# Two small VectorE jobs moved to GpSimd, and an earlier close for new VectorE cells, in a two-layer transformer kernel planned by a scheduler

**Chip, cores, metric.** One core of a Trainium2 chip. The metric is the device time of one execution in microseconds (us). "Ratio" below is the mean time of one kernel's fast runs over that of the other's of the same rounds, so it is not quite the ratio of the medians that are quoted.

## The reference

Two layers over x of 2048 rows by 512 columns; each is attention with 32 heads of 16, then an MLP of 1792 with a tanh GELU.

```python
x = x + _A_ref(_layernorm(x), A_wqkv, A_wo)              # attention
x = x + _B_ref(_layernorm(x), B_w1, B_b1, B_w2, B_b2)    # MLP
x = x + _A_ref(_layernorm(x), A_wqkv, A_wo)
x = x + _B_ref(_layernorm(x), B_w1, B_b1, B_w2, B_b2)

def _A_ref(x, wqkv, wo):                                 # cut
    scores = jnp.einsum("bhqd,bhkd->bhqk", q, k) * (Dh ** -0.5)
    p = _softmax(scores, axis=-1)
    o = jnp.einsum("bhqk,bhkd->bhqd", p, v)
    return o.transpose(...).reshape(B, S, D) @ wo
```

## The kernel before

A scheduler in the host program walks through generators ("threads") that yield operations with a modelled cost, keeps a modelled clock for each engine, and freezes one instruction order for each engine. Attention is cut into passes: eight heads' halves against a segment of 512 (at the end 256) queries. A pass has cells of 128 keys by 512 queries, in four columns (`a`). TensorE makes a cell's scores. Then either ScalarE takes the exponentials of two or three cells in one ACTIVATE, or VectorE makes one cell by an add-and-convert (`dfirst`) and two integer shifts (`dchain`): a "shift cell". Four PV matmuls use a shift cell, one uses a ScalarE cell. A pass accumulates in the one PV bank. The scheduler also books "fillers", matmuls whose result nobody uses, in gaps of TensorE.

The LN scale and shift, and the softmax normalisation at a pass's end:

```python
    def ln_tile(self, c, t, dst, dkeys, quick):
        ...
        yield _Op("dve", 0.4, lambda e: e.tensor_scalar(
            T["XLN"][:, x, :], T["X"][:, t, :], T["RSTD"][:, t:t + 1], T["NMR"][:, t:t + 1], op0=ALU.mult, op1=ALU.add),
            reads=["X.%d" % t, "RSTD.%d" % c, "NMR.%d" % c], writes=["XLN.%d" % x])
        if not quick:                       # a DMA transposes it; quick tiles go by TensorE
        ...
    def norm(self, l, seg, g, b, part, final):
        ...
        for i, t in enumerate(ts):
            o3 = T["OTT"][:, o, 0:w].rearrange("p (k c) -> p k c", c=32)[:, :, 16 * t:16 * t + 16]
            yield _Op("dve", 0.1 + 0.31 * w / 512, lambda e, i=i, o3=o3: e.tensor_tensor(
                out=o3, in0=x3[:, i * nb:i * nb + nb, 0:16],
                in1=T["RC"][:, i * nb:i * nb + nb, None].to_broadcast([128, nb, 16]), op=ALU.mult), ...)
```

Which cell VectorE gets next (`alist`, `dlist`: the pass's cells that ScalarE or VectorE may take; what is left of `dlist` when `alist` is empty goes to ScalarE too):

```python
    def next_d(self, used, start, pop=True):
        for pi in (self.pa, self.pa + 1):
            ...
            na = len(self.alist[pi])
            if pi == self.pa and na + len(self.dlist[pi]) < TAIL:      # TAIL = 10
                continue
            ...
```

An output tile of the MLP, named in the experiments:

```python
    def ytile(self, l, seg, t):
        tail = l == NL - 1 and seg[0] == self.NQ - 1
        ...
        b = None if tail else (yield ("need", ("w", l, seg, "2", (t, 0))))
        b = yield ("acq", "misc")
```

The softmax here doesn't subtract the row's maximum and nothing guards it: scores larger than these inputs give would overflow.

## Time and profile before

| before | |
|---|---|
| time | 1599.42 us (1598.87 to 1599.91, 3 runs); 1599.38 in the 6 runs beside the change |
| busy | ScalarE 1551.9 us (97%), TensorE 1431.5, VectorE 1360.6, GpSimd 115.7 |
| cells | 3221 in 1332 ACTIVATEs on ScalarE, 875 on VectorE |
| chain that ended last | ScalarE 72%, TensorE 25% |

ScalarE is the engine to watch. Its lines are in the prediction. I cut the span at its last exponential, a cut that the prediction did not make. Busy time by stretches (columns: stretch, length, then TensorE, its weight loads, VectorE, ScalarE and GpSimd busy with their instruction counts, granted clock, DMA), before:

```profile
80.00:1568.08 1488.08, 1332.56 (x17277) 410.33 (x17269) 1298.14 (x2489) 1468.96 (x1303) 89.71 (x106) 0.99 0.21 60
1568.08:1597.20 29.12, 23.33 (x530) 15.39 (x530) 8.94 (x22) 11.34 (x18) 1.07 (x2) 0.99 0.13 39
```

The span is 80 us of opening, the stretch to the last exponential (ScalarE busy 1469.0, idle 19.1 us), and a tail of 29.1 us in which TensorE has the most work. "Granted clock" is the share of its full clock that TensorE was given; what it looks like in the trace is told with the experiments.

### The profile page before, as it was taken

The page shows a single profiled execution, that of the slowest core. Times are in us where ns is not written, and L with a number is a line of the kernel's source. Part 1 is how long each engine was busy: PE and PEld are TensorE (multiplying, and loading weights), DVE is VectorE, ACT ScalarE, POOL GpSimd, SP SyncE. Part 2 cuts the span into 40 slices and gives each one's busy share as a digit, 9 for nine tenths or more (in the row PEclk, how much of TensorE's full clock was granted, in tenths as well). Part 3 has the DMA queues.
Part 4 walks back from the last instruction along what each step waited for, and adds up shares of the span by engine and source line. Part 5 has one row for each costly group of instructions (what it writes and reads, how often), then busy time and mean ns, then how long its engine had stood idle before and what let it go on. Part 6 is the DMA issues. An engine that isn't in the chain of part 4 may idle for free.

```text
span 1597.2 us, 42967 instructions
## 1 busy us (share of the span) xinstructions
PE 1431.5 (90%) x18762; PEld 449.4 (28%) x18762; DVE 1360.6 (85%) x2628; ACT 1551.9 (97%) x1391; POOL 115.7 (7%) x150
## 2 busy tenths in 40 slices
PE   8988889989899998999989988878998989888988
PEld 3222222222222222222222222222222222333344
DVE  6689998789998889978799788889878988997894
ACT  7999999999999999999999999989999999999995
POOL 4101010000000000000100010110000000000000
PEclk9999999999999999999999999999999999999999
DMA  5000001431115211142011510001251105313430
GB/s 146 15 2 1 2 14 48 133 81 41 25 50 147 60 35 28 48 146 67 28 34 41 172 41 28 1 1 34 70 170 30 33 14 156 97 35 101 140 81 29
DMA packets 141768, 96.90 MB, mean 61 GB/s; under 512 B 36877, under 2 KB 141582, under 8 KB 141582
## 3 DMA queue, kind: packets, MB, share of 16 engines
q1 hardware_dynamic: 141582, 94.14, 20.9%
q8 instruction: 150, 2.46, 0.6%
q14 instruction: 36, 0.29, 0.1%
HBM read 84.41 MB, written 2.10 MB: 54 GB/s over the span
## 4 chain that ended last, share of the span: by engine, by line
ACT 72%; PE 25%; DVE 2%; issue 0%; DMA 0%; POOL 0%; SPq 0%; ACTq 0%
ACT pt L1462 63%; PE ps L511 10%; PE ps L1134 8%; PE ps L1523 7%; ACT g L890 3%; ACT v L1462 2%; ACT kt L1462 1%; ACT q L1462 1%; ACT L890 1%; DVE du L1279 1%; ACT L1462 1%; DVE g L869 0%; PE ps L1122 0%; DVE kt L1279 0%; DMA x<-in_A_x_dram 0%
## 5 line engine op out<-in xcount | busy, mean ns | idle before, releaser
L1462 ACT ACTIVATE pt<-ps 128x1024 bf16<-128x1024 f32 (+1 forms) x1252 | 1377.9, 1260 | 16.0 <-PE ps L1134 7.3
L1134 PE MATMUL ps<-qp,kt 32*128 32x512 bf16 x4096 | 536.5, 385 | 146.9 <-ACT pt L1462 102.9
L1279 DVE TENSOR_SCALAR du<-ps 128x512 uint16<-128x512 f32 x705 | 477.5, 686 | 103.1 <-PE ps L1134 96.8
L1523 PE MATMUL ps<-pt,v 128*17 128x512 bf16 (+1 forms) x3340 | 457.0, 360 | 1.3 <-DVE du L1340 0.6
L1134 PEld LDWEIGHTS ps<-qp,kt 32*128 32x128 bf16 x4096 | 141.1, 91 | 693.2 <-ACT pt L1462 306.9
L1523 PE MATMUL ps<-du,vc 128*17 128x512 bf16 (+1 forms) x2370 | 327.9, 358 | 2.6 <-DVE du L1342 1.9
L1342 DVE TENSOR_SCALAR du<-du 128x2048 uint16<-128x2048 uint16 (+1 forms) x356 | 240.4, 680 | 1.9
L511 PE MATMUL ps<-xf,wr 128*32 128x512 bf16 (+1 forms) x2400 | 164.3, 368 | 1.1 <-DVE g L869 0.6
L1082 POOL TENSOR_SCALAR qp<-q,mask 128x512 bf16<-128x512 bf16 (+1 forms) x91 | 68.5, 753 | 1261.2 <-PE ps L1134 1252.4
L1523 PEld LDWEIGHTS ps<-pt,v 128*17 128x17 bf16 x3340 | 119.5, 89 | 118.5 <-issue 80.7
L1523 PE MATMUL ps<-du,v 128*17 128x512 bf16 (+1 forms) x790 | 149.4, 361 | 0.2 <-DVE xt L741 0.2
L1340 DVE TENSOR_SCALAR du<-du 128x1024 uint16<-128x1024 uint16 (+1 forms) x356 | 144.9, 419 | 1.8
L511 PE MATMUL ps<-wr,g 128*32 128x512 bf16 x1600 | 123.8, 382 | 4.4 <-ACT g L890 2.4
L1523 PEld LDWEIGHTS ps<-du,vc 128*17 128x17 bf16 x2370 | 91.2, 89 | 61.6 <-issue 25.8
L869 DVE TENSOR_SCALAR g<-ps,hb1t 128x512 bf16<-128x512 f32 (+1 forms) x112 | 79.9, 714 | 15.4 <-PE ps L511 13.9
L1523 PE MATMUL ps<-dh,vc 128*17 128x512 bf16 (+1 forms) x303 | 85.0, 359 | 0.0
L1279 DVE TENSOR_SCALAR dh<-ps 128x512 uint16<-128x512 f32 x90 | 61.7, 685 | 9.1 <-PE ps L1134 8.0
L511 PEld LDWEIGHTS ps<-xf,wr 128*32 128x32 bf16 x2400 | 51.1, 95 | 62.5 <-issue 34.2
L1279 DVE TENSOR_SCALAR kt<-ps 128x512 uint16<-128x512 f32 x80 | 54.9, 686 | 14.9 <-PE ps L1134 13.7
L1122 PE MATMUL ps<-vc 128*32 128x512 bf16 x564 | 60.0, 393 | 0.1
L1462 ACT ACTIVATE v<-ps 128x1536 bf16<-128x1536 f32 (+1 forms) x34 | 46.5, 1386 | 1.8 <-PE ps L1523 0.7
L1523 PEld LDWEIGHTS ps<-du,v 128*17 128x17 bf16 x790 | 37.5, 88 | 37.9 <-issue 21.1
(91 smaller groups left out, 1166.5 us busy)
## 6 DMA issues: line engine op xcount, KB each, us to landing
wr<-in_B_w_dram SPq DMA_DIRECT2D x256, 256.0 KB, 2.9
wr<-in_A_wqkv_dram SPq DMA_DIRECT2D x24, 256.0 KB, 2.9
wr<-in_A_wo_dram SPq DMA_DIRECT2D x18, 256.0 KB, 3.0
out_dram<-x SPq DMA_DIRECT2D x16, 128.0 KB, 2.7
g<-in_A_wqkv_dram SPq DMA_DIRECT2D x3, 512.0 KB, 6.0
x<-in_A_x_dram SPq DMA_DIRECT2D x3, 512.0 KB, 8.9
q<-in_B_w_dram SPq DMA_DIRECT2D x3, 512.0 KB, 5.5
kt<-in_B_w_dram SPq DMA_DIRECT2D x4, 256.0 KB, 3.5
```

The lines of the kernel that those rows point to most:

```text
L511: return [lambda e, a=a: e.matmul(out[32 * a:32 * a + 32, :], lhsT=lhsT[:, 32 * a:32 * a + 32], rhs=rhs, start=start, stop=stop, tile_posi ...
L869: yield _Op("dve", 0.21 + n / 966, lambda e, fc=fc, pb=pb: e.tensor_scalar(T["G"][:, fc, q], pb, T["HB1T"][:, fc:fc + 1], None, op0=ALU.ad ...
L890: lambda e, g=g: e.activation(out=g, in_=g, func=ACT.Gelu_apprx_tanh), reads=gk, writes=gk, prio=2)
L1082: yield _Op("pool", 0.1 + 0.6 * w / 512, lambda e, s=s, q=q, i=i, t=t, w=w: e.tensor_scalar(T["QP"][:, s, w * i:w * i + w], q, T["MASK"][: ...
L1122: fns.append(lambda e, o=o, w=w, a=a, m=m: e.matmul(o, lhsT=w, rhs=rhs, start=start, stop=start, tile_position=(0, m * a)))
L1134: return (lambda e: e.matmul(o, lhsT=lhsT, rhs=rhs, start=True, stop=True, tile_position=(32 * a, 0)), ["K%d.%d.%d" % (l, gb, kt // 4), "Q ...
L1279: yield _Op("dve", 0.68, lambda e: e.tensor_scalar(u, self.bank(b), E_SCALE, E_BIAS, op0=ALU.mult, op1=ALU.add), reads=["B.%d" % b], write ...
L1340: yield _Op("dve", 0.08 + 0.14 * n, lambda e: e.tensor_scalar(U[:, 1, 0:n, :], U[:, 0, 0:n, :], SHIFT, None, op0=ALU.add), reads=key[0], w ...
L1342: yield _Op("dve", 0.08 + 0.28 * n, lambda e: e.tensor_scalar(U[:, 2:4, 0:n, :], U[:, 0:2, 0:n, :], 2 * SHIFT, None, op0=ALU.add), reads=k ...
L1462: yield _Op("act", 0.065 + 0.4267 * n, lambda e, src=src, dst=dst: e.activation(out=dst, in_=src, func=ACT.Exp, scale=0.25), reads=["B.%d" ...
L1523: op.fns.append(lambda e, o=o, lhsT=q[0][0][m], rhs=q[0][1][:, n * m:n * m + n], a=a, st=st, sp=sp: e.matmul(o, lhsT=lhsT, rhs=rhs, start= ...
```

## The change

The intent: take two small jobs off VectorE so that it can take more cells from ScalarE, and stop shift cells from being opened late in a pass.

```diff
+OPENING = 18
-        yield _Op("dve", 0.4, lambda e: e.tensor_scalar(
+        eng, cost = ("dve", 0.4) if quick else ("pool", 0.72)
+        yield _Op(eng, cost, lambda e: e.tensor_scalar(            # LN scale and shift
...
+        pool = g < 6 and seg[2] == 512
-            yield _Op("dve", 0.1 + 0.31 * w / 512, lambda ...
+            yield _Op(*(("pool", 0.1 + 0.55 * w / 512) if pool else ("dve", 0.1 + 0.31 * w / 512)), lambda ...
...
-            if pi == self.pa and na + len(self.dlist[pi]) < TAIL:
+            left = [sum(x[2] == a for x in self.dlist[pi]) for a in range(4)]
+            if pi == self.pa and na + len(self.dlist[pi]) < (OPENING if min(left) == max(left) else TAIL):
                 continue
```

More of the change, by code (lines that the diff above doesn't have):

```diff
@@ L750, in norm @@
             o3 = T["OTT"][:, o, 0:w].rearrange("p (k c) -> p k c", c=32)[:, :, 16 * t:16 * t + 16]
-            yield _Op("dve", 0.1 + 0.31 * w / 512, lambda e, i=i, o3=o3: e.tensor_tensor(
+            yield _Op(*(("pool", 0.1 + 0.55 * w / 512) if pool else ("dve", 0.1 + 0.31 * w / 512)), lambda e, i=i, o3=o3: e.tensor_tensor(
                 out=o3, in0=x3[:, i * nb:i * nb + nb, 0:16],
```

## The prediction

> **What bounds the kernel now.** I read the page of the profile first: its busy shares, then the chain that ended last.
>
> ```profile
> PE 1431.5 (90%) x18762; PEld 449.4 (28%) x18762; DVE 1360.6 (85%) x2628; ACT 1551.9 (97%) x1391; POOL 115.7 (7%) x150
> ...
> ACT 72%; PE 25%; DVE 2%; issue 0%; DMA 0%; POOL 0%; SPq 0%; ACTq 0%
> ```
>
> ScalarE (ACT) works 97% of the span and carries 72% of the chain. GpSimd (POOL) is nearly empty. Next I cut the span into opening, middle and tail with the view of busy time by stretches (columns: PE, PEld, DVE, ACT, POOL).
>
> ```profile
> 0.00:80.00 80.00, 75.57 (x960) 23.64 (x963) 53.49 (x118) 71.57 (x72) 24.88 (x42) 1.00 0.31 80
> 80.00:1520.00 1440.00, 1290.23 (x16421) 388.67 (x16414) 1254.52 (x2398) 1420.95 (x1259) 89.71 (x106) 0.99 0.21 60
> 1520.00:1597.20 77.20, 65.67 (x1389) 37.06 (x1386) 52.56 (x114) 59.35 (x62) 1.07 (x2) 1.00 0.21 57
> ```
>
> ACT idles 8.4 us in the opening, 19.1 us in the 1440 us of the middle and 17.9 us in the tail: 45 us in all. The opening and the tail (a last MLP with no attention beside it) are not touched by the change. So the time is ACT's work plus about 45 us, and a change to another engine pays only if it takes work off ACT or shortens the 19 us. What ACT does in the middle, and what the other engines do for it, is in the groups by shape:
>
> ```profile
> L1462 ACT ACTIVATE pt<-ps 128x1024 bf16<-128x1024 f32 x763 | 802.7, 1093 | 7.2 <-PE ps L1134 4.0 <-PE ps L1523 2.0
> L1462 ACT ACTIVATE pt<-ps 128x1536 bf16<-128x1536 f32 x489 | 743.8, 1521 | 8.8 <-PE ps L1523 3.9 <-PE ps L1134 3.3
> L1279 DVE TENSOR_SCALAR du<-ps 128x512 uint16<-128x512 f32 x705 | 477.5, 686 | 103.1 <-PE ps L1134 96.8
> L1342 DVE TENSOR_SCALAR du<-du 128x2048 uint16<-128x2048 uint16 x349 | 237.4, 686 | 1.9
> L1340 DVE TENSOR_SCALAR du<-du 128x1024 uint16<-128x1024 uint16 x349 | 143.0, 422 | 1.8
> L1082 POOL TENSOR_SCALAR qp<-q,mask 128x512 bf16<-128x512 bf16 x75 | 59.5, 794 | 1074.8 <-PE ps L1134 1066.7 <-ACT q L667 7.9
> L600 DVE TENSOR_SCALAR xln<-x,rstd,nmr 128x512 bf16<-128x512 bf16 x64 | 25.7, 414 | 2.8 <-DMA kt<-xln 2.6
> L751 DVE TENSOR_TENSOR ott<-xt,rc 128x256 bf16<-128x256 f32 x56 | 23.2, 414 | 0.1
> ```
>
> There are 4096 cells of scores (128 keys by 512 queries). Each cell's exponential is made either by ACT (two or three cells per ACTIVATE) or by VectorE (DVE), with one add-and-convert from PSUM (L1279) and a share of two shift instructions (L1340, L1342) for the "shift cells". A scheduler in the host program decides cell by cell who takes it, from modelled costs and readiness. So freeing DVE pays by one road: the scheduler gives DVE more cells, and ACT has fewer. I counted the instructions of the two built programs, which is no timing. Before: 775 ACTIVATEs of two cells and 557 of three, so 3221 cells in 1332 instructions, and 875 on DVE. After: 793 of two, 540 of three and one of one, so 3207 cells in 1334 instructions, and 889 on DVE.
>
> [...] an undisturbed L1082 of 512 columns takes 0.69 us in the timeline. [...]
>
> [...] the same L1082 takes 0.69 us at 141 us and 2.07 us at 157 us, and its mean is 794 ns.
>
> ```profile
> 141.23 0.69 POOL L1082 TENSOR_SCALAR qp<-q,mask 128x512 bf16<-128x512 bf16 x1 [14.90 <-PE ps L1134]
> 157.10 2.07 POOL L1082 TENSOR_SCALAR qp<-q,mask 128x512 bf16<-128x512 bf16 x1 [15.18 <-PE ps L1134]
> ```
>
> [...]
>
> **The change, part by part.**
>
> (1) LN scale and shift to GpSimd. By the counts 58 of 64 L600 leave DVE: 58 x 0.414 = 24.0 us less on DVE, and 58 x 0.70 = 41 us more on GpSimd (estimate from L1082, same shape, one input). The six that stay are the quick ones at the start and the very end.
>
> (2) Softmax normalisation. 42 of the 56 L751 of 256 columns leave DVE: 42 x 0.414 = 17.4 us[...]. Passes 6 and 7 of a segment, behind which the output projection waits, and the half segments stay on DVE, so no longer latency stands where a segment ends. GpSimd goes from 116 to some 185 to 200 us, 12% of the span: it can't be a bound.
>
> (3) DVE takes 14 more cells: 14 x 0.686 = 9.6 us. By the counts the shift instructions become 3 more pairs (3 x 1.11 us) and 8 more singles (8 x 0.71 us): 9.0 us. DVE's sum: -41.4 + 18.6 = -23 us, so about 1338 us busy, with a lower share than now.
>
> (4) ACT, which decides. The slope from the two rows above: 1521 - 1093 = 428 ns per cell. All that ACT does besides exponentials (GELUs 53 us, 16 table loads of 1.283 us, some 8 us of copies) is about 82 us, so the exponentials take 1551.9 - 82 = 1470 us; less 3221 x 0.428 = 1379 us this leaves 91 us over 1332 instructions, 0.068 us each. The change is then -14 x 0.428 + 2 x 0.068 = **-5.9 us** on ACT. That lies on the path almost whole, since ACT is never out of work for long.
>
> (5) The opening rule. A DVE cell of the current pass may now be opened, when the four columns are level, only with 18 or more cells of the pass left, not 10. I built the two halves alone and counted. GpSimd's part alone puts 3205 cells in 1344 ACTIVATEs: -16 x 0.428 + 12 x 0.068 = -6.0 us. The opening rule alone gives ACT 9 cells more, in 3 instructions more: +4.1 us. Together they are worth the same as GpSimd's part alone, with 10 fewer ACTIVATEs and 2 cells more. So the rule buys nothing on ACT's work; if it buys anything, it is ACT's waits. A cell opened late holds the pass's single PV bank until its shift chain is done, so that PV matmuls and, behind them, the buffers that ACT writes into are late. Such waits are few: in ACT's waits between 30 and 1560 us, these two carry nearly all.
>
> ```profile
> ACT pt L1462 <- PE ps L1134: 7.3, 18, 0.8
> ACT pt L1462 <- PE ps L1523: 5.9, 3, 3.7
> ```
>
> The second is the kind the rule can help, 5.9 us in three waits. I take 1.5 us off, a choice, not a reckoning.
>
> (6) PE. Each cell on DVE needs four PV matmuls where one on ACT needs one: 42 more column matmuls, at 1431 / 18762 = 0.076 us about 3 us. Against it, 112 filler matmuls (L1122[...]) fall away, about 8.5 us. PE is 90% busy but loses work on balance, so it does not become the bound.
>
> Sum: 1599.4 - 5.9 - 1.5 = **1592 us**, 0.5% faster.
>
> **Rivals.**
>
> A. [...] For: shift instructions run 493 us (all shapes of L1340 and L1342), 31% of the span, 974 of them, so 0.61 start each us. [...] A delayed shift chain delays PV, and a delayed L1279 delays the score bank. Against: DVE loses 23 us of work[...]; it has 15% idle[...]. [...]
>
> B. *New waits of the frozen order.* Nearly every row of the order of instructions moves, so the 19 us of idle in the middle is drawn anew. GpSimd in its order serves the masked queries (L1082), which the next pass needs, behind an xln that itself may wait for statistics or its transpose's buffer. One such pile-up costs 1 to 3 us (the longest ACT wait now is 3.7 us). [...] Against: queries are made a pass or more ahead (three buffers). This makes 1592 plus or minus 5.
>
> C. *The rule works better than I grant*: it removes most of the 15 us that ACT waits in the middle, and frees PE. For: PE fillers fall from 1076 to 964 with both parts, while GpSimd's part alone keeps 1020, so the plan has fewer PE gaps. Against: fillers are not waits of ACT. It would give about 1584 us.
>
> **Range and chances.** The count of cells is sure, its price is measured, so -5.9 us is firm within 0.5 us; the rest is idle time on ACT, from -8 us (C) to +8 us (A with B). The eight-in-ten range is 1585 to 1599 us. Faster by over 2% would need 1567 us, more than all the idle time of the middle; slower by over 2% would need 38 us of new idle time on ACT. Both are very unlikely: 0.01 each, and 0.98 for within 2%.
>
> **What would show it.** Right: ACT busy near 1546 us, idle 42 to 45 us; DVE near 1338 us[...]; GpSimd 185 to 205 us; L600 on GpSimd at 0.70 to 0.95 us mean; ACT's wait for L1523 under 5.9 us. Wrong: ACT's idle time in the middle over 25 us with waits for the score matmuls L1134 that DVE releases (A); waits for L1082's queries (B); idle under 12 us (C); GpSimd's normalisation at over 1.2 us mean (my estimate of step 2 off, though it would not matter for the time).

Cuts are marked; what they took is not shown by a trace or a run of this case. GpSimd's "185 to 200 us" came from 116 + 41 for the LN operations + 27 for the 42 normalisations (42 times the 0.65 us that the scheduler books for each, in the diff, is the same 27 us). Rival A is that moved work and VectorE's shift instructions, when they run beside each other, slow each other so much that the gain goes. Its result of near 1600 us and the +8 us of the range are the author's estimate. So is rival B's 1 to 3 us, taken from the longest wait of 3.7 us.

## The result, and the profile after

1590.1 us (1588.9 to 1594.27, 6 runs) against 1599.38 us: ratio 0.9946, interval 0.9932 to 0.9959. Within 2%, 0.5% faster, inside the range.

The page of the kernel after, busy times and chain:

```profile
PE 1424.2 (90%) x18701; PEld 444.6 (28%) x18701; DVE 1352.0 (85%) x2564; ACT 1547.1 (97%) x1393; POOL 200.5 (13%) x250
...
ACT 67%; PE 29%; DVE 2%; POOL 1%; issue 1%; DMA 0%; ACTq 0%; POOLq 0%
```

The same cut at the last exponential, after:

```profile
80.00:1560.83 1480.83, 1326.71 (x17240) 407.01 (x17241) 1294.49 (x2438) 1464.20 (x1305) 166.43 (x194) 0.99 0.21 60
1560.83:1587.30 26.47, 22.29 (x520) 14.13 (x512) 8.94 (x22) 11.34 (x18) 1.07 (x2) 1.00 0.14 42
```

The span is 9.9 us shorter: 4.8 us less ScalarE work, 2.5 us less ScalarE idle time (16.6 against 19.1), and 2.6 us less tail (profiled at clocks of 0.994 and 0.995). The tail was not in the prediction. Groups by shape, after (L1466, L1346, L1344 and L1085 are L1462, L1342, L1340 and L1082 of before):

```profile
L1466 ACT ACTIVATE pt<-ps 128x1024 bf16<-128x1024 f32 x769 | 798.2, 1080 | 7.4 <-PE ps L1137 6.0
L1466 ACT ACTIVATE pt<-ps 128x1536 bf16<-128x1536 f32 x491 | 740.2, 1507 | 7.8 <-PE ps L1137 4.2 <-PE ps L1527 1.3
L1346 DVE TENSOR_SCALAR du<-du 128x2048 uint16<-128x2048 uint16 x350 | 241.2, 693 | 2.5
L1344 DVE TENSOR_SCALAR du<-du 128x1024 uint16<-128x1024 uint16 x350 | 147.9, 433 | 2.0
L602 POOL TENSOR_SCALAR xln<-x,rstd,nmr 128x512 bf16<-128x512 bf16 x58 | 58.2, 1008 | 33.3 <-DMA xf<-xln 23.2 <-DVE nmr L591 8.8 <-DVE mv L583 1.0
L754 POOL TENSOR_TENSOR ott<-xt,rc 128x256 bf16<-128x256 f32 x42 | 29.5, 703 | 178.5 <-DVE rc L746 178.5
```

GpSimd's mean times, 1008 and 703 ns, lie above the shortest, 762 and 618 ns (by tile). The difference goes with VectorE's shift instructions. Of the 58 L602, the 24 with none beside them took 762 to 777 ns, though other VectorE work ran beside them for 0.65 us on average; the 34 that had one took 763 to 1907 ns, mean 1176. On VectorE, the 286 of the 2048-column L1346 written to `du` with no GpSimd instruction beside them took 682 ns on average, the 64 with one 742, up to 1107. The add-and-convert (L1283 into `du`) took 685 ns either way. ("Beside" is an overlap of over 20 ns in the packed trace.) This is called the slowdown below; the names of e7 and e8 call it the lock, and its cause is not shown here. On average the shift instructions grew a little, 686 to 693 and 422 to 433 ns: part of the slowdown, at least, lies inside the busy records of both engines (sized under e3 and e4). Of L602's shape, L1085 took 0.69 us at the shortest, with one scalar for each partition where L602 has two. ScalarE's waits after, between 30 and 1550 us:

```profile
ACT pt L1466 <- PE ps L1137: 10.3, 25, 0.9
ACT pt L1466 <- PE ps L1527: 1.3, 1, 1.3
```

With `pt` written, the waits for PV matmuls, L1523 before, fell from 5.9 to 1.3 us; those for scores rose from 7.3 to 10.3 us. (The table below counts all tiles that ScalarE writes: 6.6 to 1.3.)

What such a PV wait is, can be read at 1054 us of the kernel before (timeline; other lines cut):

```profile
1053.84 0.42 DVE L1342 TENSOR_SCALAR dh<-dh 128x1024 uint16<-128x1024 uint16 x1
1054.64 0.59 PE L1523 MATMUL ps<-dh,vc 128*17 128x512 bf16 x1
1055.03 0.63 PE L1523 MATMUL ps<-dh,vc 128*17 128x512 bf16 x1
1055.70 0.69 DVE L737 TENSOR_TENSOR v<-v,ps 128x512 f32<-128x512 f32 x1 [0.65 <-PE ps L1122]
1056.45 1.16 PE L1523 MATMUL ps<-pt,v 128*17 128x512 bf16 x9
1057.62 1.45 ACT L1462 ACTIVATE pt<-ps 128x1536 bf16<-128x1536 f32 x1 [3.65 <-PE ps L1523]
```

A single late cell (`dh`) ends its shifts at 1054.3 us. Its matmuls close the pass, VectorE empties the PV bank (L737), only then the next pass's PV matmuls run, and ScalarE, which had no free buffer to write into, starts 3.65 us late.

Not all of the 3.65 us is the plan's. TensorE's granted clock was 0.50 just then (third number from the end), and the two closing matmuls took 0.59 and 0.63 us. In e3 below, which has the same program on ScalarE and TensorE, the clock was 1.00 at this place, the same two took 0.39 and 0.38 us, and the wait was 2.42 us. Stretches of before, then of e3, and e3's wait:

```profile
1053.90:1057.20 3.30, 3.30 (x25) 1.11 (x28) 2.65 (x7) 0.07 (x1) 0.00 (x0) 0.50 0.00 0
1053.00:1057.00 4.00, 3.35 (x38) 1.14 (x39) 3.73 (x9) 1.58 (x3) 0.20 (x1) 1.00 0.01 4
1056.79 1.45 ACT L1467 ACTIVATE pt<-ps 128x1536 bf16<-128x1536 f32 x1 [2.42 <-PE ps L1528]
```

### The profile page after: what moved, and what is told of

It reads as the page before. It is cut to its first block, busy times and chain, and to the rows that moved or that the text cites. A ratio compares the mean times of both kernels' runs of the same rounds, so it can differ in the third digit from the quotient of the medians.

```text
span 1587.3 us, 42896 instructions
## 1 busy us (share of the span) xinstructions
PE 1424.2 (90%) x18701; PEld 444.6 (28%) x18701; DVE 1352.0 (85%) x2564; ACT 1547.1 (97%) x1393; POOL 200.5 (13%) x250
## 4 chain that ended last, share of the span: by engine, by line
ACT 67%; PE 29%; DVE 2%; POOL 1%; issue 1%; DMA 0%; ACTq 0%; POOLq 0%
ACT pt L1466 60%; PE ps L512 11%; PE ps L1137 9%; PE ps L1527 8%; ACT g L893 3%; ACT v L1466 2%; ACT kt L1466 1%; ACT q L1466 1%; DVE du L1283 1%; ACT L893 1%; ACT L1466 0%; DMA xf<-xln 0%; PE ps L1125 0%; POOL xln L602 0%; POOL rstd L588 0%
## 5 line engine op out<-in xcount | busy, mean ns | idle before, releaser
L1466 ACT ACTIVATE pt<-ps 128x1536 bf16<-128x1536 f32 (+2 forms) x1261 | 1384.2, 1246 | 15.2 <-PE ps L1137 10.3
L1283 DVE TENSOR_SCALAR du<-ps 128x512 uint16<-128x512 f32 x711 | 479.7, 685 | 97.5 <-PE ps L1137 89.6
L1527 PE MATMUL ps<-pt,v 128*17 128x512 bf16 (+1 forms) x3368 | 433.8, 359 | 2.3 <-ACT pt L1466 0.8
L1527 PE MATMUL ps<-du,vc 128*17 128x512 bf16 (+1 forms) x2394 | 333.8, 358 | 2.7 <-DVE du L1346 1.4
L1346 DVE TENSOR_SCALAR du<-du 128x2048 uint16<-128x2048 uint16 x361 | 246.3, 687 | 2.5
L1085 POOL TENSOR_SCALAR qp<-q,mask 128x512 bf16<-128x512 bf16 (+1 forms) x91 | 66.3, 728 | 1013.8 <-PE ps L1137 1005.1
L512 PE MATMUL ps<-xf,wr 128*32 128x512 bf16 (+1 forms) x2400 | 170.8, 368 | 1.7 <-DMA xf<-xln 1.1
L1344 DVE TENSOR_SCALAR du<-du 128x1024 uint16<-128x1024 uint16 x361 | 150.5, 428 | 2.0
L1527 PEld LDWEIGHTS ps<-pt,v 128*17 128x17 bf16 x3368 | 111.8, 89 | 113.0 <-issue 72.9
L512 PE MATMUL ps<-wr,g 128*32 128x512 bf16 x1600 | 123.8, 384 | 5.5 <-ACT g L893 5.0
L1283 DVE TENSOR_SCALAR dh<-ps 128x512 uint16<-128x512 f32 x96 | 65.8, 685 | 11.5 <-PE ps L1137 10.8
L1283 DVE TENSOR_SCALAR kt<-ps 128x512 uint16<-128x512 f32 x82 | 56.1, 684 | 20.7 <-PE ps L1137 19.9
L512 PEld LDWEIGHTS ps<-xf,wr 128*32 128x32 bf16 x2400 | 53.6, 95 | 61.5 <-issue 33.5
L602 POOL TENSOR_SCALAR xln<-x,rstd,nmr 128x512 bf16<-128x512 bf16 x58 | 58.2, 1008 | 33.3 <-DMA xf<-xln 23.2
L754 POOL TENSOR_TENSOR ott<-xt,rc 128x256 bf16<-128x256 f32 x42 | 29.5, 703 | 178.5 <-DVE rc L746 178.5
L1125 PE MATMUL ps<-vc 128*32 128x512 bf16 x476 | 50.9, 395 | 0.1
```

The costliest lines, as they stand in the source:

```text
L512: return [lambda e, a=a: e.matmul(out[32 * a:32 * a + 32, :], lhsT=lhsT[:, 32 * a:32 * a + 32], rhs=rhs, start=start, stop=stop, tile_posi ...
L602: yield _Op(eng, cost, lambda e: e.tensor_scalar(T["XLN"][:, x, :], T["X"][:, t, :], T["RSTD"][:, t:t + 1], T["NMR"][:, t:t + 1], op0=ALU. ...
L1085: yield _Op("pool", 0.1 + 0.6 * w / 512, lambda e, s=s, q=q, i=i, t=t, w=w: e.tensor_scalar(T["QP"][:, s, w * i:w * i + w], q, T["MASK"][: ...
L1125: fns.append(lambda e, o=o, w=w, a=a, m=m: e.matmul(o, lhsT=w, rhs=rhs, start=start, stop=start, tile_position=(0, m * a)))
L1283: yield _Op("dve", 0.68, lambda e: e.tensor_scalar(u, self.bank(b), E_SCALE, E_BIAS, op0=ALU.mult, op1=ALU.add), reads=["B.%d" % b], write ...
L1344: yield _Op("dve", 0.08 + 0.14 * n, lambda e: e.tensor_scalar(U[:, 1, 0:n, :], U[:, 0, 0:n, :], SHIFT, None, op0=ALU.add), reads=key[0], w ...
```

## The experiments

Within one kernel's runs, the time follows the mean granted clock: before, 33 runs, 0.75 us for each 0.001 of clock (so some 0.8 us for each 3.4 us at half clock, an estimate from this slope and the span); GpSimd's part alone (e2), 1.02. The clock was not the same in every run (0.990 to 0.996 in those 33), so the table also gives each kernel's time on its own fitted line at clock 0.994 (a calculation; root mean square residual 0.3 to 1.1 us). Busy, idle and tail are from the profiled run, with the cut at the last exponential; "PV" is the part of idle that waits for PV matmuls.

| | cells / ACTIVATEs | ratio to before (95%) | at 0.994 | ScalarE busy, idle (PV) | tail |
|---|---|---|---|---|---|
| before | 3221 / 1332 | 1 | 1600.0 | 1469.0, 19.1 (6.6) | 29.1 |
| e1 rule alone | 3230 / 1335 | 1.0010 (0.9997-1.0023) | 1602.0 | 1473.8, 19.8 (6.2) | 26.4 |
| e2 GpSimd alone | 3205 / 1344 | 0.9993 (0.9978-1.0008) | 1598.1 | 1465.7, 23.6 (5.1) | 30.7 |
| e3 old plan, moved | 3221 / 1332 | 0.9993 (0.9981-1.0005) | 1599.2 | 1469.0, 18.8 (5.3) | 29.1 |
| e4 new plan, not moved | 3207 / 1334 | 0.9961 (0.9949-0.9972) | 1592.3 | 1465.5, 19.5 (1.3) | 26.5 |
| e5 before, end reordered | 3221 / 1332 | 0.9989 (0.9976-1.0002) | 1598.5 | 1469.5, 19.7 (6.6) | 27.0 |
| e6 e2, end reordered | 3205 / 1344 | 0.9967 (0.9954-0.9980) | 1596.4 | 1465.3, 19.5 (5.1) | 26.8 |
| **after** | 3207 / 1334 | 0.9946 (0.9932-0.9959) | 1589.2 | 1464.2, 16.6 (1.3) | 26.5 |
| e7 after, one more product for each moved operation | 3207 / 1334 | 0.9944 (0.9932-0.9956) | 1591.1 | 1465.2, 18.2 (1.3) | 26.5 |
| e9 rule at 14 | 3206 / 1337 | 0.9952 (0.9939-0.9965) | 1591.6 | 1464.7, 19.5 (3.7) | 26.2 |
| e10 rule at 16 | 3204 / 1342 | 0.9971 (0.9957-0.9985) | 1594.4 | 1463.6, 21.7 (7.2) | 26.5 |
| e11 rule at 24 | 3218 / 1331 | 0.9954 (0.9941-0.9968) | 1592.4 | 1468.0, 15.5 (1.6) | 26.5 |
| e12 all norms moved | 3194 / 1346 | 0.9948 (0.9934-0.9961) | 1588.3 | 1461.0, 23.8 (0.8) | 26.8 |

In the packed traces the granted clock is 1.0 but for a few stretches of 3.4 us, or multiples of it, at 0.5. Between 80 us and the last exponential they add up to 17.1 us in the profile of before, 27.3 in that of e2 and 10.2 in that of e6, though e2 and e6 have the same program there. So the idle times of the table are at each profile's own clock. Outside these stretches ScalarE idles 14.3 us before, 18.3 in e2, 18.4 in e6, 15.8 in e4 and 13.2 after (sums over the packed traces). Two cautions go with the column at 0.994: a plan can move the clock itself (e8's runs lie at 0.962 and 0.963, those of the whole change at 0.988 to 0.995), and that share of its effect is taken out; and the six runs of the whole change are of an earlier batch than the others.

### e1 and e2: each part alone

```diff
 e1: the lines of OPENING and `left`, nothing else
 e2: the lines of "pool" in ln_tile and norm, nothing else
```

> Only the opening rule, LN scale and normalisation stay on VectorE. By its instruction counts ScalarE has 3230 cells in 1335 ACTIVATEs, 9 cells and 3 instructions more than before: +4.1 us of ScalarE work. Theory (the time is ScalarE's cells plus its waits, and the rule acts on waits only): 1599.4 + 4.1 less at most some 2 us of waits = 1601 to 1604 us. Rival (the rule pays by itself, with shorter waits of ScalarE): under 1599 us, with ScalarE idle under 40 us.

> Only the move to GpSimd, the old opening rule. By its counts ScalarE has 3205 cells in 1344 ACTIVATEs: -16 x 0.428 + 12 x 0.068 = -6.0 us of ScalarE work. Theory: 1593.4 us if ScalarE's waits stay as before, and the rest of the way to the 1590.1 us of the whole change is what the rule gives. Rival (the rule gives nothing): 1590 us, with ScalarE idle 40 us as in the whole change. Rival (waits are drawn anew with each order): anything from 1589 to 1598, with no pattern in the waits.

Measured: e1 1601.89 us, as expected: 4.9 us more ScalarE work, the PV waits almost as before, the tail 2.7 us shorter. e2 **1600.38 us**, with no gain that the interval can tell from none, where 1593.4 was the sum, 1590 the first rival and 1589 to 1598 the second; none of the three held. Its runs range from 1595.2 us (clock 0.997) to 1603.8 (0.989). At equal clock the parts are worth -1.9 and +2.0 us, their sum about nothing, and together they are worth -10.8 (by the ratios, without the clock: -1.1, +1.6 and -8.6). In e2's own stretches 3.2 of the promised 6.0 us of work are gone, but the idle time and the tail are longer:

```profile
80.00:1569.37 1489.37, 1342.13 (x17290) 410.33 (x17290) 1296.85 (x2440) 1465.74 (x1314) 167.34 (x194) 0.99 0.21 60
1569.37:1600.10 30.73, 24.93 (x524) 16.27 (x518) 8.93 (x22) 11.46 (x18) 1.07 (x2) 0.94 0.12 37
```

(The tail's 30.7 us was at clock 0.94 in that stretch; the order in it is that of before. Of the idle time, 5.3 us lie at half clock, against 4.8 before; outside it e2 still idles 4.0 us more.) The LN half and the normalisation half of the move were not separated: a build with the LN half alone was refused by the simulator, and so was one with the rule at 20. That stays open.

### e3 and e4: the plan and the move apart

```diff
-            ev = self.P.group(e, op.fns, ...)                # issue where it is booked
+            ev = self.P.group(op.real or e, op.fns, ...)     # book on one engine, issue on another
 e3: kernel before, booked on "dve", op.real = "pool" for the 58 + 42 operations
 e4: kernel after, booked on "pool", op.real = "dve" for the same
```

> The plan of before, instruction for instruction on ScalarE and TensorE (3221 cells in 1332 ACTIVATEs), but the 58 LN scale-and-shifts and 42 normalisations are issued on GpSimd; the scheduler still books them on VectorE, so it gives VectorE no cell more. VectorE is 41 us lighter, nothing else changes. Theory (the gain comes through cells): 1597 to 1600 us. Rival (a lighter VectorE shortens the waits by itself): 1590 to 1594 us. Rival [...]: over 1601 us.

(The second rival: the slowdown costs time.)

> The plan of the whole change, instruction for instruction on ScalarE and TensorE (3207 cells), but the 58 and 42 operations run on VectorE, in the place where GpSimd would have been given them. VectorE carries 41 us more than it was planned for, near 1393 us or 88%. Theory (ScalarE's cells decide and VectorE has slack): 1592 to 1597 us, the 5.9 us less part eaten by late VectorE work. Rival (VectorE's lighter load is itself needed, its lateness reaches ScalarE at full): 1600 us and more.

Measured: e3 1600.16 us, e4 1594.21 us, e4 inside what the theory said, e3 0.2 us above its 1597 to 1600. ScalarE's and TensorE's programs are unchanged in each, so e3 shows that a VectorE with 41 us less to do is worth 0.2% at most by itself (the interval's lower end), and e4 that the new plan keeps most of its gain (-7.7 of -10.8 us at equal clock, though e4's runs lie at clocks of 0.989 to 0.992 and its value at 0.994 is extrapolated; -6.2 of -8.6 by the ratios) even where VectorE still does everything. **Most of the gain lies in the plan, not in the relief.** The page of e3:

```profile
PE 1431.2 (90%) x18762; PEld 448.8 (28%) x18762; DVE 1337.2 (84%) x2528; ACT 1552.1 (97%) x1391; POOL 199.1 (12%) x250
```

VectorE's busy time fell by 23.4 us where 41.4 were taken away. The other 18 us are not all slowdown. Busy time counts a moment in which two records overlap once; added up one by one (count times mean, from the groups by shape) VectorE's records fall from 1512.0 to 1476.4 us, by 35.6. So records that stayed grew by some 6 us, 5.4 of them in the 974 shift instructions; the other 12 us are overlap that went with the moved records. e4 against the change says the same: with the same 996 shift instructions, their records add up to 509.9 us in e4 and 517.2 with the moved work on GpSimd. The slowdown that VectorE's records show is thus 5 to 7 us. (e4's VectorE was busy 1374.1 us, not the 1393 expected, which reckoned without the overlap.)

### e5 and e6: the order at the end

Where does the shorter tail come from? TensorE's first work after the last exponential, before, in the timeline (other engines and the PV matmuls cut):

```profile
1569.07 1.05 PE L511 MATMUL ps<-wr,otn 128*32 128x512 bf16 x12
1571.21 1.48 PE L511 MATMUL ps<-q,g 128*32 128x512 bf16 x24 [1.09 <-ACT g L890]
1572.50 0.62 PE L511 MATMUL ps<-wr,otn 128*32 128x512 bf16 x8
...
1575.31 2.78 PE L511 MATMUL ps<-q,g 128*32 128x512 bf16 x48
...
1580.04 0.91 PE L611 MATMUL ps<-ident,xln 128*128 128x128 bf16 x8 [1.31 <-DVE xln L600]
```

And after:

```profile
1561.31 1.04 PE L512 MATMUL ps<-wr,otn 128*32 128x512 bf16 x12
1563.67 1.05 PE L512 MATMUL ps<-wr,otn 128*32 128x512 bf16 x16 [1.33 <-DVE otn L759]
1564.53 2.78 PE L512 MATMUL ps<-q,g 128*32 128x512 bf16 x48
...
1569.62 0.62 PE L613 MATMUL ps<-ident,xln 128*128 128x128 bf16 x8
```

Before, an output tile of the segment before (`q,g`) waits for its GELU between the parts of the last output projection (`wr,otn`), which holds up the last LN; then TensorE has nothing left to do in that LN and waits. After, the projection comes first and an output tile fills the LN's time: the transposes start 8.8 us after the last exponential, against 12.0 us. The experiments force that order on the kernel before and on e2:

```diff
     def ytile(self, l, seg, t):
+        if tail and seg != self.segs[l][-1]:
+            for u in self.tiles(self.segs[l][-1]):
+                yield ("need", ("xready", u, 2 * l + 1))
```

> The kernel before with one thing changed: the output tiles of the second-last segment may start only when the last segment's attention is added to x. Up to the last exponential the program is that of before; after it, TensorE does both tiles of the last output projection first and fills the last LN's wait with an output tile, the order that the whole change and the rule alone have (26.5 us from the last exponential to the end, against 29.1 before). Theory (the rule's gain at the end is this order and nothing else): 2.6 us less than before, ratio 0.9984, tail 26.5 us. Rival (the tail is shorter because the rule ends the last pass's VectorE cells earlier): no change, tail 29 us.

> GpSimd's part alone (as in the second experiment) with the same forced order at the end. Theory: 4 us less than that run's 1600.4 us, so 1596 to 1597 us, tail 26.5 us; the further 6 to 7 us to the whole change are then shorter waits of ScalarE before its last exponential and depend on the plan. Rival (the tail is made of TensorE work that moves elsewhere): 1599 to 1601 us.

Measured: e5 1598.38 us, e6 1594.29 us. The tails:

```profile
1569.22:1596.20 26.98, 22.69 (x526) 14.65 (x526) 8.94 (x22) 11.34 (x18) 1.07 (x2) 1.00 0.14 42
```

for e5, and for e6

```profile
1564.77:1591.60 26.83, 22.66 (x520) 14.56 (x514) 8.94 (x22) 11.34 (x18) 1.06 (x2) 1.00 0.14 42
```

The order of the end is worth some 2 us: 29.1 to 27.0 us in the tail, and 1.5 to 1.7 us of the time at equal clock. e5's interval alone does not exclude no effect; the stretches do show it. Half of e6's 6 us below e2 is clock (means of 0.995 and 0.992). The order does not belong to the rule as such: builds with the rule at 16 and 24 have the old order at the end, those at 14 and 18 the new one (read off the builds; 14, 16 and 24 were run with the order forced only). e6's tail was 26.8 us, against 26.5 expected.

### e7 and e8: more work on GpSimd beside VectorE

```diff
+            if e == "pool" and op.writes[0][:3] in ("XLN", "OTT") and "B2row" in self.P.lastw:
+                for _ in range(1):       # e8: range(4)
+                    self.P.group("pool", [lambda e: e.tensor_tensor(out=self.scr[:, :], in0=self.b2[:, 0:192],
+                                 in1=self.b2[:, 192:384], op=ALU.mult)], reads=["B2row"], writes=["SCR"])
```

> The whole change, and behind each of the 100 moved operations GpSimd does one further product of two SBUF operands (192 columns, estimate 0.5 us from the 0.62 us that the 256-column normalisation takes) into a scratch tile nobody reads. All other engines' programs are the same. GpSimd gains 50 us busy. Theory (VectorE has slack[...]): within 1 us of the whole change, 1589 to 1592 us. Rival [...] 1595 us.

> As the one before, with four such products behind each moved operation: GpSimd gains some 200 us and works 400 us in all, 25%. Theory (swallowed): 1590 to 1595 us, with some delay of queries behind the burst of 2 us. Rival [...] 1610 us.

(The theories say that VectorE's slack swallows the slowdown, the rivals that it reaches ScalarE. The delays that the rivals' times came from are author's estimates, not shown.)

Measured: e7 1591.67 us (ratio to before 0.9944, as the whole change; at equal clock 1.9 us above it); e8 **1690.89 us**, which neither expectation held. The pages of e7, then of e8:

```profile
PE 1425.2 (90%) x18701; PEld 445.4 (28%) x18701; DVE 1360.4 (86%) x2564; ACT 1548.1 (97%) x1393; POOL 260.5 (16%) x350
```

```profile
PE 1461.2 (86%) x18701; PEld 447.5 (26%) x18701; DVE 1385.9 (82%) x2564; ACT 1554.1 (92%) x1393; POOL 442.5 (26%) x650
```

In e7, 60 us more on GpSimd put 8.4 us more into VectorE's busy time and nothing clear into the time; up to 2 us are not excluded. In e8, 242 us more put 34 us into VectorE, which can't make 100 us. What did is in TensorE's waits of e8:

```profile
PE ps L518 <- DMA xf<-xln: 58.4, 12, 8.4
```

L518 is the projection and MLP helper. After, it waits 1.1 us for this transpose (group of L512 on the page). The products stand between the four LN tiles in GpSimd's order: from the first tile's start to the fourth's it takes 10.2 to 15.6 us where the change takes 4.7 to 7.8. TensorE's frozen order stops at the matmul that needs them, up to 8.4 us at a time, with the scores for ScalarE behind it. The clock does the rest: after eleven of these twelve waits began, a stretch at half clock followed within 0.8 to 4.4 us (in the twelfth the clock was low already), and e8 spends 116 us of ScalarE's main stretch at half clock where the change spends 17. Of ScalarE's 103 us of idle time there, 65 lie at half clock. So the added work cost little as slowdown (e7) and much as latency, once it was later than the plan allows (e8).

### e9 to e12: neighbours of the rule, and more work for GpSimd

```diff
 e9, e10, e11: OPENING = 14, 16, 24, with the end's order forced (in the kernel after, forcing it changes no instruction)
 e12: pool = g < 8            # was: g < 6 and seg[2] == 512; rule at 18, end's order forced
```

> The whole change with the opening rule at 14 cells left in place of 18, and the end in the forced order (which the whole change has by itself). By counts 3206 cells in 1337 ACTIVATEs, the ScalarE work of GpSimd's part alone within 0.1 us. All times here at a mean granted clock of 0.994, to which the runs so far are brought by their own slope of some 0.7 us for 0.001. Theory S (the rule shortens ScalarE's waits in step with how early it closes): between the 1596.4 us of rule 10 and the 1589.2 us of rule 18, so 1591 to 1595 us. Rival L (each plan draws its waits anew, 18 was a good draw): anywhere from 1588 to 1599 us, out of order with the rule at 16.

> As the one before with the rule at 16: 3204 cells in 1342 ACTIVATEs, 0.6 us less ScalarE work than rule 10. Theory S: at or below the run with 14 and above rule 18, 1589 to 1593 us. Rival L: anywhere from 1588 to 1599 us.

> As before with the rule at 24: 3218 cells in 1331 ACTIVATEs, 4.7 us more ScalarE work than rule 10 and 4.5 us more than rule 18. Theory S: waits no longer than with 18, so 1592 to 1594.5 us. Rival L: 1591 to 1602 us.

> The whole change with the normalisation of every pass on GpSimd (also passes 6 and 7 of a segment and the half segments), rule at 18, end in the forced order. By counts 3194 cells in 1346 ACTIVATEs: 13 cells less than the whole change, -13 x 0.428 + 12 x 0.068 = -4.7 us of ScalarE work. Theory (cells decide, if the waits stay): 1585 to 1588 us, faster than both kernels. Rival (longer latency of the normalisation before the output projection and at the very end, and waits drawn anew): 1589 to 1596 us.

Measured: 1593.02, 1596.67, 1593.22 and 1593.36 us; the first three expectations are for equal clock. With the same end, the times at equal clock for the rule at 10 (e6), 14, 16, 18 and 24 are 1596.4, 1591.6, 1594.4, 1589.2 and 1592.4. Rule 16 came out behind 14, with 7.2 us of PV waits, so the theory that waits shrink in step with the rule falls as it was put. The rival, that each plan draws its waits anew, is not refuted; 18 is the best of five. Something of the rule may remain: at 18 and 24 with the move, PV waits are 0.8 to 1.6 us (after, e4, e7, e11, e12, of three different plans), at 10 to 16 they are 3.7 to 7.2; but the rule at 18 without the move has 6.2 (e1). Which of the two it is stays open.

e12 has 13 cells less on ScalarE and 3.2 us less work, and 7.2 us more idle time (waits for scores 18.0 us against 10.7); of the 7.2, 2.7 lie at half clock. Its median is above that of the whole change, its ratio the same. No version clearly faster than the change was found. So the theory of cells (1585 to 1588) missed and the rival (1589 to 1596) held. (Its 1588.3 at clock 0.994 hangs on six runs between 0.991 and 0.993; with the 0.75 us of before as slope it would be 1590.7.)

## Why the prediction was right, and where it was not

- **The road by cells: right, a little large.** ScalarE's work fell by 4.8 us where -5.9 was reckoned. Three profiles with the same ScalarE program (after, e4, e7) gave 1464.2 to 1465.5, so -3.5 to -4.8: "firm within 0.5 us" was too sure. A fit over the profiles up to e12, without e8, gives 0.37 us a cell and 0.11 an ACTIVATE, in place of the 0.428 and 0.068 worked out from means; the means also hold what overlaps with other records (before, ScalarE's records add up to 1774.7 us, its busy time is 1551.9).
- **"The opening and the tail ... are not touched by the change": wrong.** The tail lost 2.6 us through another order in it (e5, e6). This is the step that failed; its size, by the forced order, is about 2 us.
- **The rule, "1.5 us off": mis-sized, and GpSimd's part alone was taken to be worth its cells.** Alone it measured 1600.4 us, at equal clock -1.9 us and not -6.0. With the rule, the same end and the same work within 1.1 us, the plan is some 7 us faster at equal clock (e6 to after). Outside half clock ScalarE idles 5.2 us less (18.4 to 13.2), and 3.8 us of PV waits are the part that the profiles name; the mechanism given for it, a late cell that holds the PV bank, is read in one such wait and not isolated in a run. Why this plan has the shorter waits stays open.
- **Rival A, the slowdown: real, and swallowed.** VectorE's records show 5 to 7 us (e3, e4); the estimate that it was priced by is cut. That its busy time, 1352.0 us, lies 14 us above the 1338 reckoned is not the slowdown alone: the 1338 took the moved records off at full length, without their overlap. One more product behind each moved operation changed nothing clear (e7, ratio 0.9944 against 0.9946).
- **Rival B, waits drawn anew: stronger than I made it.** Five plans with the same end lie 7 us apart.
- The checks: ScalarE 1547.1 (near 1546 said), idle 40.2 (42 to 45 said), GpSimd 200.5 (185 to 205 said), ScalarE's wait for L1523 1.3 (under 5.9 said). L602 took 1008 ns, above the 700 to 950 said; the shortest of them took 762.

So the sum was right, in part by luck, with errors that offset each other: less gained from work than said (4.8 us, not 5.9), more from idle time and tail (5.1 us, not 1.5).

## What to carry to other kernels

When a scheduler freezes the order of a kernel whose main engine is 97% busy, price a change by that engine's work first, but test each part alone: here the parts were worth about nothing singly and some 9 to 11 us together, and each change of the plan changed the waits with it. Relief of an engine that does not bound was worth 0.2% at most until its time was given to work of the one that does (e3). Before a single long wait is put down to the plan, look at the granted clock in that stretch. Cut the span at the bounding engine's last main instruction and read the order of what follows; it can hide microseconds that no part of the change aims at.
